# First batch's scores with tokens on partitions, its softmax without VectorE transposes, a float8 step that GpSimd may take

## The chip, the cores and the metric

The kernel runs on one core of a Trainium2 chip. The metric is the device time of one execution in microseconds (us). TensorE (PE), VectorE (DVE), ScalarE (ACT) and GpSimd (POOL) compute; SyncE (SP) issues the transfers. PEld stands for TensorE's loading of weights, which the profile lists apart from its matmuls.

## The reference

An attention block with 32 state tokens for each head feeds two MLPs. Sizes: 4 batches, 8 heads, 512 tokens, head width 64; then 2176 rows of 512, a first MLP of width 2048 and a second of width 1536.

```python
scores = scale * np.matmul(x, state.transpose(0, 1, 3, 2))
scores = scores - scores.max(-1, keepdims=True)
a = np.exp(scores)
a /= a.sum(-1, keepdims=True) + 1e-09
xread = np.matmul(a, state)
scores2 = scale * np.matmul(state, x.transpose(0, 1, 3, 2))
...
sread = np.matmul(a2, x)
x = concatenate([xread, sread])          # per head, then heads side by side
h = x @ w_in
g = np.where(h >= 1, h, np.where(h <= -1, 0.0, (h + 1) ** 2 / 4.0))
y = g @ w_out
out = ((y @ w_a) * (y @ w_b)) @ w_out2
```

All arrays are float32 or wider; the weights reach the chip as 8-byte words.

## The kernel before, in words

**Arithmetic.** A float32 operand is split into a rounded part (`hi`) and the rest (`lo`), both of the type float32r, and a product is made of three matmuls, hi·hi, hi·lo and lo·hi (`three`, `mms`, L378 to L393). Plain float32 matmuls are issued for the small products: scores, transposes, and the products with the state; the trace shows each of those as two matmuls and two weight loads. The two MLPs use a seven-product scheme of Strassen's kind.

**Weights.** `conv_steps` (L404) loads a block of 8-byte words and makes float32 of it in three steps: `copy` takes one byte of each word, a second step converts that byte through float8 (`upper` in the changed kernel; here always an ACT instruction), and `join` puts the bits together on DVE. For the first MLP's input weights, 512 columns (`c0`, `c1`) or 1024 columns (`c2` and all later ones) are converted at a time.

**Attention, batch 0.** Two head groups, `k` = 0 and 1, of four heads each. `a_qk(k)` makes the scores with the 32 state tokens on partitions. `a_soft(k)` (L619) is the softmax over the 32 states: DVE transposes the scores in 32x32 blocks (L635), takes the maximum (L636), POOL subtracts it (`spread`, L628), ACT exponentiates (L360), DVE sums (L639), adds 1e-9 (L642) and inverts (L647), POOL multiplies (L628), DVE transposes back (L649), ACT makes `hi` and DVE `lo` (L653). The same scores give the second softmax, over the tokens: `s_soft` (L704), `s_tr` (transposes by TensorE, L757) and `s_read` (L772). `w_steps` (L664) makes the product of state and input weights, which takes the place of `xread @ w_in`: the product of attention and that is the first MLP's hidden layer, six matmuls of 512 columns for each of its 16 row blocks `f` (`h_mm`, L813, traced at L385). `gate` applies the activation on ACT, POOL or ACT, and DVE.

**Order.** Every operation is recorded in `Flow.op` with costs for each engine that may do it, and `Flow.order` (L95) lays them out: the engine that can start first takes, of what is ready, the operation whose due time (`late`) is earliest, and the table `NUDGE` shifts the due times of single operations and excludes engines for some. TensorE's operations keep the order of the code unless they are marked `loose`. Each engine works through its own list in order. In `phase_one` (L1346) the head of batch 0 is written out by hand: while `flow.row` is a dictionary, operations of one engine are chained in that written order. `warm` (L864) issues matmuls whose result nobody reads: 11 at the start, then `FILL` = 12 and 10.

**Banks.** Eight PSUM banks: 0 to 3 for hidden blocks (the ring `four`), 4 and 5 together are the tile `lower` (scores), 6 and 7 the tile `upper` (state times weights).

Of the kernel before, what the change touches and what calls it, by code (L numbers as in the profile page):

```python
# [9 lines left out]
F32 = mybir.dt.float32  # L10
# [3 lines left out]
ALU = mybir.AluOpType  # L14
# [6 lines left out]
    64: (119,), 65: (2433,), 72: (638,), 78: (-4.5,), 79: (20.5, "POOL"), 90: (-9.5,), 92: (658.5,), 100: (78,),  # L21
    109: (-9,), 138: (69,), 163: (-32,), 196: (-9,), 219: (-12.5,), 304: (7.5,), 328: (6, "ACT"), 1010: (33,),
    1011: (30.5,), 1092: (10,), 1094: (-1.5,), 1096: (10,), 1103: (5.5,), 1138: (-5.5,), 1170: (10,),
    1172: (191.5,), 1182: (-1,), 1201: (-5,), 1208: (29.5,), 1211: (27,), 1213: (10.5,), 1217: (8,), 1235: (-4.5,),
    1278: (9.5,),
# [175 lines left out]
def attention_then_two_mlps(  # L201
# [116 lines left out]
    def bank(b):  # L318
        return ("P", b, b + 1)
# [84 lines left out]
    def conv_steps(src, k, stage, z, dst=None, by=("ACT",)):  # L404
# [28 lines left out]
        def copy(e):  # L433
# [4 lines left out]

        t = 0.18 + 0.00116 * n
# [5 lines left out]
            lambda: act(to, z, n, AF.Copy, regs(z), regs(z), t=t, saturate=False),  # L445
# [149 lines left out]
    def a_qk(k):  # L595
# [15 lines left out]
        op({"PE": 1.05}, emit, regs(d["st"], d["xld"]), [bank(b)], loose=k > 1)  # L611
# [7 lines left out]
    def a_soft(k, sub=("POOL",), mult=("POOL",), low=("DVE", "POOL")):  # L619
        d = qs[k]  # L620
        t1, b = d["t1"], sbank[k]
# [3 lines left out]
        def spread(engs, alu, v):  # L625
            op(
                {x: {"DVE": 0.7, "POOL": 1.1}[x] for x in engs},
                lambda e: eng(e).tensor_tensor(g32(t1()), g32(t1()), b32(v()), alu),  # L628
                regs(t1, v),
                regs(t1),  # L630
                port=True,
            )

        return [
            lambda: op({"DVE": 0.72}, lambda e: nc.vector.transpose(t1(), banks[b]), [bank(b)], regs(t1)),  # L635
            lambda: op({"DVE": 0.69}, lambda e: nc.vector.reduce_max(mx(), g32(t1()), axis=AX.X), regs(t1), regs(mx)),  # L636
            lambda: spread(sub, ALU.subtract, mx),
# [10 lines left out]
            lambda: spread(mult, ALU.mult, sm),  # L648
            lambda: op({"DVE": 0.71}, lambda e: nc.vector.transpose(d["at"](), t1()), regs(t1), regs(d["at"])),  # L649
            lambda: hi_of(hi, d["at"], 512, regs(d["at"]), regs(hi)),  # L650
# [3 lines left out]
                regs(d["at"], hi),  # L654
                regs(lo),
                port=True,
            ),
        ]

    def w_state(*args):  # L660
# [933 lines left out]
```

## Time and profile before

| | |
|---|---|
| median of 3 runs | 712.39 us (711.58 to 712.58) |
| the profiled execution | 711.84 us, of which 710.1 us are its span |
| TensorE matmul busy | 697.3 us, 98% of the span |
| TensorE weight loads busy | 653.9 us |
| VectorE, ScalarE, GpSimd busy | 556.5, 421.1, 105.3 us |
| mean granted TensorE clock | 0.998 of full speed |

Busy time is the time in which an engine had an instruction under way. In the page's 40 slices TensorE is at 9 tenths in every slice but the first (7) and the last (7), so what it does not do lies almost all in the first 18 us and some stretches behind them. "Idle before" in a row is the time that the engine stood still ahead of that instruction, and the name behind the arrow is what released it.

### The profile page before, as it was taken

The numbers are of one execution on the slowest core, as the hardware profiler recorded it, in microseconds if no ns is written. First come the engines' busy times: TensorE is split into PE (matmuls) and PEld (weight loads), VectorE is DVE, ScalarE is ACT, GpSimd is POOL, SyncE is SP. The second block draws the span as 40 slices with busy tenths as digits, with TensorE's granted clock in tenths as the row PEclk, the third lists the DMA queues.
The fourth block names the chain that finished last, engine by engine and source line by source line (L and its number), as shares of the span: only waits on it lengthen the run. The fifth ranks groups of instructions, "written<-read, shape, count | busy, mean of one in ns | idle before, by whom it ended". The sixth has DMA issues, their size and how long they took to land.

```text
span 710.1 us, 12246 instructions
## 1 busy us (share of the span) xinstructions
PE 697.3 (98%) x4818; PEld 653.9 (92%) x4818; DVE 556.5 (78%) x701; ACT 421.1 (59%) x622; POOL 105.3 (15%) x75
## 2 busy tenths in 40 slices
PE   7799999999999999999999999999999999999997
PEld 6366767889999999999999999999999999999997
DVE  6898879898997787899998686756536888987760
ACT  4888888697445455666666666455325536544440
POOL 3445768792000000000000000000000000000000
PEclk9999999999999999999999999999999999999999
DMA  8879977395674165142445767363631348454201
GB/s 345 346 247 325 330 279 264 104 386 162 207 252 150 63 196 190 54 143 106 135 149 178 243 221 245 117 195 109 203 135 42 106 145 287 127 174 146 79 30 44
DMA packets 75449, 128.92 MB, mean 182 GB/s; under 512 B 5632, under 2 KB 51200, under 8 KB 75392
## 3 DMA queue, kind: packets, MB, share of 16 engines
q1 hardware_dynamic: 75392, 128.15, 53.7%
q8 instruction: 37, 0.61, 0.3%
q14 instruction: 20, 0.16, 0.1%
HBM read 84.87 MB, written 43.25 MB: 180 GB/s over the span
## 4 chain that ended last, share of the span: by engine, by line
PE 89%; DMA 4%; DVE 3%; ACT 2%; issue 1%; POOL 0%; DVEq 0%; POOLq 0%; ACTq 0%
PE bank L385 82%; PE bank L843 2%; PE upper L674 2%; DMA f<-in_w_dram 2%; DMA g_d<-fs 1%; PE lower L772 1%; DMA f<-g_d 1%; ACT f L360 1%; PE bank L867 1%; DVE f L918 1%; DVE rh L370 1%; DVE r L370 1%; DMA f<-x_d 0%; PE lower L540 0%; PE lower L757 0%
## 5 line engine op out<-in xcount | busy, mean ns | idle before, releaser
L385 PE MATMUL bank<-rh,r 128*128 128x352 f32 (+2 forms) x1398 | 222.4, 316 | 0.9 <-ACT f L360 0.5
L385 PEld LDWEIGHTS bank<-rh,r 128*128 128x128 f32 x1398 | 215.9, 189 | 1.7 <-DVE rh L370 0.7
L360 ACT ACTIVATE f<-bank 128x368 f32<-128x368 f32 (+3 forms) x183 | 82.4, 454 | 124.5 <-PE bank L385 123.7
L385 PE MATMUL bank<-r,r 128*128 128x368 f32 (+1 forms) x960 | 156.2, 315 | 0.0
L385 PEld LDWEIGHTS bank<-r,r 128*128 128x128 f32 x960 | 147.8, 188 | 0.1
L360 ACT ACTIVATE rh<-f 128x736 fp32r<-128x736 f32 (+5 forms) x120 | 100.4, 846 | 75.8 <-PE bank L385 65.7
L370 DVE TENSOR_TENSOR f<-bank,f 128x368 f32<-128x368 f32 (+2 forms) x168 | 85.8, 517 | 72.3 <-PE bank L385 68.0
L370 DVE TENSOR_TENSOR rh<-f,rh 128x736 fp32r<-128x736 f32 (+5 forms) x120 | 119.2, 1002 | 25.5 <-ACT rh L360 25.0
L385 PE MATMUL bank<-r 128*128 128x512 f32 (+1 forms) x582 | 121.1, 360 | 4.5 <-ACT r L360 2.0
L385 PEld LDWEIGHTS bank<-r 128*128 128x128 f32 x582 | 94.7, 190 | 30.0 <-issue 8.4
L370 DVE TENSOR_TENSOR r<-f,r 128x768 fp32r<-128x768 f32 (+6 forms) x85 | 94.3, 1122 | 15.6 <-ACT r L360 15.6
L360 ACT ACTIVATE r<-f 128x768 fp32r<-128x768 f32 (+6 forms) x85 | 80.2, 953 | 39.7 <-PE bank L385 17.9
L385 PE MATMUL bank<-rh 128*128 128x352 f32 (+2 forms) x564 | 93.5, 318 | 0.1
L385 PEld LDWEIGHTS bank<-rh 128*128 128x128 f32 x564 | 88.4, 189 | 1.2 <-DVE f L370 0.6
L918 DVE TENSOR_TENSOR f<-f 128x256 f32<-128x256 f32 (+6 forms) x106 | 83.3, 804 | 6.1 <-DMA f<-p_d 5.0
L385 PE MATMUL bank<-r,rh 128*128 128x368 f32 (+1 forms) x480 | 80.3, 315 | 0.0
L385 PEld LDWEIGHTS bank<-r,rh 128*128 128x128 f32 x480 | 74.3, 188 | 0.0
L360 ACT ACTIVATE f<-f 128x1024 fp8e5<-128x1024 f32 (+1 forms) x43 | 48.0, 1122 | 2.0 <-POOL f L437 1.7
L435 ACT ACTIVATE f<-f 128x512 fp8e5<-128x512 fp8e5 (+1 forms) x28 | 28.1, 1004 | 20.3 <-DMA f<-in_w_dram 14.6
L448 DVE SCALAR_TENSOR_TENSOR f<-f 128x1024 uint32<-128x1024 uint32 (+1 forms) x34 | 34.0, 999 | 6.9 <-ACT f L360 6.8
L793 ACT ACTIVATE f<-bank,half 128x512 f32<-128x512 f32 x40 | 27.4, 691 | 9.1 <-PE bank L385 5.5
L807 DVE SCALAR_TENSOR_TENSOR f<-f,bank 128x512 f32<-128x512 f32 x40 | 26.5, 678 | 4.9 <-ACT f L800 3.5
(65 smaller groups left out, 432.8 us busy)
## 6 DMA issues: line engine op xcount, KB each, us to landing
f<-in_w_dram SPq DMA_DIRECT2D x25, 1024.0 KB, 6.2
f<-g_d SPq DMA_DIRECT2D x36, 368.0 KB, 4.9
f<-p_d SPq DMA_DIRECT2D x17, 768.0 KB, 4.9
g_d<-f SPq DMA_DIRECT2D x40, 256.0 KB, 5.1
f<-in_w_dram SPq DMA_DIRECT2D x18, 512.0 KB, 4.1
p_d<-f SPq DMA_DIRECT2D x48, 184.0 KB, 2.0
g_d<-fs SPq DMA_DIRECT2D x28, 256.0 KB, 4.8
f<-g_d SPq DMA_DIRECT2D x16, 352.0 KB, 4.7
```

The source lines that it names most:

```text
L360: lambda e: nc.scalar.activation(dst(), src(), func, **{k: (v() if callable(v) else v) for k, v in kws.items()}),
L370: op({"DVE": t_tt(n)}, lambda e: nc.vector.tensor_tensor(dst(), a(), b(), alu), rd, wr, port=port)
L385: nc.tensor.matmul(o, w, x, start=first and k == 0, stop=last and k == n - 1, skip_group_check=onto)
L435: nc.scalar.activation(to(), of(), AF.Copy, saturate=False)
L448: lambda e: nc.vector.scalar_tensor_tensor(out(U32), words_of(1, U32)(), 5, z(U32), ALU.logical_shift_right, ALU.bitwise_or),
L674: nc.tensor.matmul(banks[ab[q]][o : o + NS, :cols].rearrange("p (f x) -> p f x", x=P), st[q]()[64 * h : 64 * h + 64, NS * j : NS * j + NS] ...
L772: nc.tensor.matmul(banks[4][64 * e2 : 64 * e2 + 64, o : o + NS], xn()[:, c * 256 + p * 128 + e2 * 64 : c * 256 + p * 128 + (e2 + 1) * 64], ...
L793: lambda e: nc.scalar.activation(g(), h(), AF.Relu, bias=half[:, 0:1], scale=0.5),
L807: lambda e: nc.vector.scalar_tensor_tensor(g(), g(), 1.0, h(), ALU.min, ALU.max),
L843: nc.tensor.matmul(banks[b][:, P * i : P * i + P], w[:, P * c : P * c + P], xs()[:, P * c : P * c + P], start=c == 0, stop=c == 3,)
L867: nc.tensor.matmul(banks[3][:, :128], ident, ident, start=True, stop=True)
L918: lambda e: eng(e).tensor_tensor(dst(), a(), b(), alu),
```

## The change

Scores of batch 0 are also made with the tokens on partitions, by a new function `t_qk(k)`: for `k` = 0 eight matmuls of 64 moving columns, for `k` = 1 sixteen of 32 columns, all with 128x128 weights taken from `x`. They go to banks 0 and 1. The softmax reads them there: the maximum and the subtraction are DVE instructions with a PSUM operand, both `STREAM_TRANSPOSE` pairs are gone, the multiplication may be DVE's or POOL's, and the way back is four TensorE transposes for each `k` (`back`), after which `hi` and `lo` read PSUM. `a_qk(0)` and `a_qk(1)` stay, for the second softmax. The float8 step may be done by POOL wherever the copy step lists POOL. `flow.row` is `None`, so the head's order comes from due times; the hand-written list is changed, `NUDGE` is another table, and the ring `four` starts with bank 2.

```diff
 NUDGE = {
-    64: (119,), 65: (2433,), 72: (638,), 78: (-4.5,), 79: (20.5, "POOL"), 90: (-9.5,), 92: (658.5,), 100: (78,),
...
+    24: (136,), 30: (31.5,), 31: (29,), 32: (16.5,), 36: (63,), 37: (70,), 39: (19,), 40: (29.5,),
...
+        def upper(e):
+            if e == "ACT":
+                nc.scalar.activation(to(), z(), AF.Copy, saturate=False)
+            else:
+                eng(e).tensor_copy(to(), z(), saturate=False)
...
-            lambda: act(to, z, n, AF.Copy, regs(z), regs(z), t=t, saturate=False),
+            lambda: op({x: c for x, c in (("ACT", t), ("POOL", 0.2 + 0.0012 * n)) if x == "ACT" or x in by}, upper, regs(z), regs(z), port=True),
...
-        op({"PE": 1.05}, emit, regs(d["st"], d["xld"]), [bank(b)], loose=k > 1)
+        op({"PE": 0.55}, emit, regs(d["st"], d["xld"]), [bank(b)], loose=True)
+
+    def t_qk(k):
+        d = qs[k]
+
+        def emit(e):
+            for c in range(4):
+                for j in range(0, 4, 2 - k % 2):
+                    o, m = P * c + NS * (j ^ (k % 2)), NS * (2 - k % 2)
+                    nc.tensor.matmul(
+                        banks[k][:, o : o + m],
+                        d["xld"]()[:, 512 * (j // 2) + P * c : 512 * (j // 2) + P * c + P],
+                        d["st"]()[:, NS * j : NS * j + m],
+                        start=True,
+                        stop=True,
+                    )
+
+        op({"PE": 1.1}, emit, regs(d["st"], d["xld"]), [bank(k)])
...
+        def back(e):
+            for c in range(4):
+                nc.tensor.transpose(banks[k][:, P * c : P * c + P], t1()[:, P * c : P * c + P], ident)
...
-            lambda: op({"DVE": 0.72}, lambda e: nc.vector.transpose(t1(), banks[b]), [bank(b)], regs(t1)),
-            lambda: op({"DVE": 0.69}, lambda e: nc.vector.reduce_max(mx(), g32(t1()), axis=AX.X), regs(t1), regs(mx)),
-            lambda: spread(sub, ALU.subtract, mx),
...
+            lambda: op(
+                {"DVE": 0.66}, lambda e: nc.vector.reduce_max(mx(), g32(banks[k]), axis=AX.X), [bank(k)], regs(mx)
+            ),
+            lambda: op(
+                {"DVE": 0.68},
+                lambda e: nc.vector.tensor_tensor(g32(t1()), g32(banks[k]), b32(mx()), ALU.subtract),
+                [bank(k)] + regs(mx),
                 regs(t1),
-                port=True,
-            )
...
-            lambda: spread(mult, ALU.mult, sm),
-            lambda: op({"DVE": 0.71}, lambda e: nc.vector.transpose(d["at"](), t1()), regs(t1), regs(d["at"])),
-            lambda: hi_of(hi, d["at"], 512, regs(d["at"]), regs(hi)),
...
+            lambda: op({"PE": 0.5}, back, regs(t1), [bank(k)], loose=True),
+            lambda: hi_of(hi, lambda: banks[k], 512, [bank(k)], regs(hi)),
+            lambda: tt(lo, lambda: banks[k], lambda: hi(F32), ALU.subtract, 512, [bank(k)] + regs(hi), regs(lo)),
...
-    four, six = Ring([0, 1, 2, 3]), Ring([4, 5, 6, 7, 2, 3] * 2 + [6, 7, 2, 3])
+    four, six = Ring([2, 3, 0, 1]), Ring([4, 5, 6, 7, 2, 3] * 2 + [6, 7, 2, 3])
...
-        a_qk(0)
-        a_qk(1)
...
+        t_qk(0)
+        t_qk(1)
...
-        flow.row = {}
+        flow.row = None
...
-            s0[tr], s0[mx], s0[sub], s1[tr], s1[mx], s1[sub], c0[copy], s0[exp], c0[byte], s1[exp], s0[sm], c0[join],
...
+            s0[mx], s0[sub], s1[mx], s1[sub], c0[copy], s0[exp], c0[byte], s1[exp], s0[sm], s0[eps], s0[rec], s0[mult],
+            c0[join], lambda: a_qk(0), lambda: a_qk(1), v0[prod], s0[back], lambda: warm(FILL[1]), c1[copy], v0[top], v0[top1],
```

What this does to the order. The first place is TensorE's list from its first instruction to the first hidden block. Before (L867 is `warm`, L603 `a_qk`, L674 the product of state and weights, L385 a hidden block):

```order
L867 MATMUL bank_70<-ident 128x128 x11
L603 MATMUL lower<-fs 32x512 x8
L867 MATMUL bank_70<-ident 128x128 x12
L674 MATMUL upper<-fs 32x128 x8
L867 MATMUL bank_70<-ident 128x128 x10
L385 MATMUL bank_67<-r_65 128x512 x6
```

Now (L890 is `warm`, L608 `a_qk`, L625 `t_qk`, L697 the product of state and weights, L649 `back`, L384 a hidden block; banks 67 to 70 are banks 0 to 3):

```order
L890 MATMUL bank_70<-ident 128x128 x11
L608 MATMUL lower<-fs 32x512 x4
L625 MATMUL bank_67<-fs 128x64 x8
L608 MATMUL lower<-fs 32x512 x4
L625 MATMUL bank_68<-fs 128x32 x16
L890 MATMUL bank_70<-ident 128x128 x12
L697 MATMUL upper<-fs 32x128 x8
L890 MATMUL bank_70<-ident 128x128 x10
L649 MATMUL bank_68<-ident,fs 128x128 x4
L649 MATMUL bank_67<-ident,fs 128x128 x4
L384 MATMUL bank_69<-r_65 128x512 x6
```

Both `t_qk` stand ahead of the first fill, and each behind the `a_qk` of its group; `back` stands between the second fill and the first hidden block.

The second place is TensorE's list behind that, around the first transposes of the second softmax (`s_tr`, L757 before). Before:

```order
L674 MATMUL upper<-fs 32x128 x8
L385 MATMUL bank_68<-r_65 128x512 x6
L674 MATMUL upper<-fs 32x256 x8
L385 MATMUL bank_69<-r_65 128x512 x6
L674 MATMUL upper<-fs 32x512 x8
L385 MATMUL bank_70<-r_65 128x512 x6
L757 MATMUL lower<-ident,fs 128x128 x4
L385 MATMUL bank_67<-r_65 128x512 x6
L757 MATMUL lower<-ident,fs 128x128 x4
```

Now (`s_tr` is L780):

```order
L697 MATMUL upper<-fs 32x128 x8
L384 MATMUL bank_70<-r_65 128x512 x6
L697 MATMUL upper<-fs 32x256 x8
L780 MATMUL lower<-ident,fs 128x128 x4
L697 MATMUL upper<-fs 32x512 x8
L780 MATMUL lower<-ident,fs 128x128 x4
L384 MATMUL bank_67<-r_65 128x512 x6
L384 MATMUL bank_68<-r_65 128x512 x6
```

Both `s_tr` have moved ahead of the third hidden block; before, two blocks stood ahead of the first of them and three ahead of the second.

The third place is DVE's list at the head. Before (L635 and L649 are the transposes, L636 the maximum, L639 the sum, L448 `join`, L642 and L647 the small steps, L370 `lo` of state times weights):

```order
L635 STREAM_TRANSPOSE fs<-lower 128x512
L636 TENSOR_REDUCE fs<-fs 128x16
L635 STREAM_TRANSPOSE fs<-lower 128x512
L636 TENSOR_REDUCE fs<-fs 128x16
L639 TENSOR_REDUCE fs<-fs 128x16
L448 SCALAR_TENSOR_TENSOR fs<-f_66 128x512
L642 TENSOR_SCALAR fs<-fs 128x16
L647 RECIPROCAL fs<-fs 128x16
L639 TENSOR_REDUCE fs<-fs 128x16
```

Now (L653 is the maximum, L657 the subtraction, L453 `join`, L662 the sum, L665 and L670 the small steps):

```order
L653 TENSOR_REDUCE fs<-bank_67 128x16
L657 TENSOR_TENSOR fs<-bank_67,fs 128x512
L653 TENSOR_REDUCE fs<-bank_68 128x16
L657 TENSOR_TENSOR fs<-bank_68,fs 128x512
L453 SCALAR_TENSOR_TENSOR fs<-f_66 128x512
L662 TENSOR_REDUCE fs<-fs 128x16
L665 TENSOR_SCALAR fs<-fs 128x16
L662 TENSOR_REDUCE fs<-fs 128x16
L665 TENSOR_SCALAR fs<-fs 128x16
L670 RECIPROCAL fs<-fs 128x16
```

`join` of the first weights, on which the first product of state and weights waits, stands behind the second group's subtraction, as it stood behind the second group's maximum and the first group's sum before.

## Rows read from the trace of the kernel before

**Rows 1.** The page, busy time, share and instructions of each engine.

```profile
PE 697.3 (98%) x4818; PEld 653.9 (92%) x4818; DVE 556.5 (78%) x701; ACT 421.1 (59%) x622; POOL 105.3 (15%) x75
```

**Rows 2.** TensorE's waits, first 60 us: waiting, releaser, total us, times, longest.

```profile
PE bank L385 <- ACT r L360: 2.0, 3, 0.8
PE bank L385 <- DVE r L370: 1.6, 2, 0.9
...
PE lower L757 <- ACT fs L740: 1.0, 1, 1.0
PE bank L385 <- DVE r L653: 0.9, 1, 0.9
PE lower L603 <- DVE fs L635: 0.8, 1, 0.8
PE upper L674 <- DVE fs L448: 0.4, 1, 0.4
```

**Rows 3.** Windows: length, busy us of PE, PEld, DVE, ACT, POOL, clock, DMA.

```profile
15.00:20.00 5.00, 3.04 (x24) 1.52 (x24) 5.00 (x7) 3.65 (x7) 3.18 (x2) 1.00 1.03 396
20.00:25.00 5.00, 2.88 (x24) 1.47 (x25) 4.07 (x10) 4.88 (x9) 1.36 (x2) 1.00 1.03 411
25.00:30.00 5.00, 4.97 (x26) 1.96 (x24) 3.94 (x5) 3.03 (x4) 1.35 (x1) 0.66 1.03 410
```

**Rows 4.** Timeline of TensorE: start us, us, instruction, idle before and releaser.

```profile
5.53 1.06 PE L603 MATMUL lower<-fs 64*32 64x512 f32 x8
...
11.73 0.45 PE L674 MATMUL upper<-fs 64*32 64x128 f32 x16 [0.36 <-DVE fs L448]
...
20.46 1.19 PE L385 MATMUL bank<-r 128*128 128x512 f32 x4 [0.76 <-DVE r L370]
...
24.64 1.75 PE L385 MATMUL bank<-r 128*128 128x512 f32 x4 [0.87 <-DVE r L370]
26.32 1.96 PE L674 MATMUL upper<-fs 64*32 64x512 f32 x16
...
33.67 1.09 PE L674 MATMUL upper<-fs 64*32 64x512 f32 x16
```

**Rows 5.** Weight loads by shape, whole span: busy us, mean ns of one.

```profile
L843 PEld LDWEIGHTS bank<-fs 128*128 128x128 f32 x128 | 14.6, 192 | 1.8 <-issue 1.7
...
L772 PEld LDWEIGHTS lower<-fs 128*64 128x64 f32 x256 | 7.8, 138 | 2.4 <-ACT fs L360 1.7 <-ACT r L360 0.4 <-issue 0.4
```

**Rows 6.** Small float32 matmuls by shape, whole span: busy us, mean ns.

```profile
L843 PE MATMUL bank<-fs 128*128 128x128 f32 x128 | 15.0, 277 | 0.0
...
L772 PE MATMUL lower<-fs 128*64 128x32 f32 x256 | 8.2, 223 | 0.5 <-ACT fs L360 0.5
L757 PE MATMUL lower<-ident,fs 128*128 128x128 f32 x32 | 4.7, 279 | 1.1 <-ACT fs L740 1.0
```

**Rows 7.** Timeline of DVE at the head.

```profile
6.66 0.72 DVE L635 STREAM_TRANSPOSE fs<-lower 128x512 f32<-128x512 f32 x1 [3.63 <-PE lower L603]
7.42 0.69 DVE L636 TENSOR_REDUCE fs<-fs 128x16 f32<-128x512 f32 x1
...
11.60 0.16 DVE L642 TENSOR_SCALAR fs<-fs 128x16 f32<-128x16 f32 x1
...
12.63 0.65 DVE L642 TENSOR_SCALAR fs<-fs 128x16 f32<-128x16 f32 x1
```

**Rows 8.** Timeline of POOL at the head.

```profile
8.18 1.05 POOL L628 TENSOR_TENSOR fs<-fs 128x512 f32<-128x512 f32 x1 [6.88 <-DVE fs L636]
...
14.70 1.35 POOL L437 COPY f<-f 128x1024 uint8<-128x1024 uint8 x1
```

**Rows 9.** Timeline of ACT: first softmax's exponentials, a scaling of the second.

```profile
9.26 0.63 ACT L360 ACTIVATE fs<-fs 128x512 f32<-128x512 f32 x1 [0.63 <-POOL fs L628]
...
11.16 0.63 ACT L360 ACTIVATE fs<-fs 128x512 f32<-128x512 f32 x1 [0.59 <-POOL fs L628]
...
29.30 0.71 ACT L740 ACTIVATE fs<-fs 128x512 f32<-128x512 f32 x1
```

More of the change, by code (lines that the diff above doesn't have):

```diff
@@ L20 @@
 NUDGE = {
-    64: (119,), 65: (2433,), 72: (638,), 78: (-4.5,), 79: (20.5, "POOL"), 90: (-9.5,), 92: (658.5,), 100: (78,),
[L22 to L25, printed above, removed]
+    24: (136,), 30: (31.5,), 31: (29,), 32: (16.5,), 36: (63,), 37: (70,), 39: (19,), 40: (29.5,),
+    47: (-98.5, "POOL"), 54: (-5,), 58: (-55,), 66: (128,), 90: (-31,), 108: (4,), 122: (-3.5,), 137: (9.5, "DVE"),
+    142: (36,), 185: (18.5,), 224: (7.5,), 312: (16,), 647: (3, "POOL"), 1010: (27.5,), 1011: (23,), 1076: (6.5,),
+    1091: (-9.5,), 1110: (3,), 1138: (-8,), 1205: (-5,), 1211: (0.5,), 1261: (10,), 1263: (2.5,),
 }
@@ L647, in a_soft @@
             lambda: op({"DVE": 0.25}, lambda e: nc.vector.reciprocal(sm(), sm()), regs(sm), regs(sm), port=True),
[L648 to L650 removed]
             lambda: op(
[L652 to L655 removed]
+                {"DVE": 0.7, "POOL": 1.1},
+                lambda e: eng(e).tensor_tensor(g32(t1()), g32(t1()), b32(sm()), ALU.mult),
+                regs(t1, sm),
+                regs(t1),
                 port=True,
             ),
+            lambda: op({"PE": 0.5}, back, regs(t1), [bank(k)], loose=True),
+            lambda: hi_of(hi, lambda: banks[k], 512, [bank(k)], regs(hi)),
+            lambda: tt(lo, lambda: banks[k], lambda: hi(F32), ALU.subtract, 512, [bank(k)] + regs(hi), regs(lo)),
         ]
@@ L1361, in phase_one @@
         warm(WARM)
-        a_qk(0)
-        a_qk(1)
-        s0 = a_soft(0, ("POOL",), ("POOL",), ("DVE",))
-        s1 = a_soft(1, ("POOL",), ("POOL",), ("DVE",))
+        t_qk(0)
+        t_qk(1)
+        s0, s1 = a_soft(0), a_soft(1)
         first_w.append(len(flow.ops))
         v0, v1, v2 = w_steps(0, 0, 0, 1), w_steps(0, 0, 1, 2), w_steps(0, 0, 2, 4)
-        flow.row = {}
-        tr, mx, sub, exp, sm, eps, rec, mult, back, high, low = range(11)
+        flow.row = None
+        mx, sub, exp, sm, eps, rec, mult, back, high, low = range(10)
         copy, byte, join = range(3)
@@ L1373, in phase_one @@
         for f in (
-            s0[tr], s0[mx], s0[sub], s1[tr], s1[mx], s1[sub], c0[copy], s0[exp], c0[byte], s1[exp], s0[sm], c0[join],
-            s0[eps], s0[rec], s0[mult], v0[prod], lambda: warm(FILL[1]), c1[copy], v0[top], v0[top1], c1[byte],
-            s1[sm], s1[eps], s1[rec], s1[mult], v0[rest], v0[rest1], s0[back], s0[high], s1[back], s1[high], s0[low],
-            c2[copy], s1[low], c1[join], c2[byte],
+            s0[mx], s0[sub], s1[mx], s1[sub], c0[copy], s0[exp], c0[byte], s1[exp], s0[sm], s0[eps], s0[rec], s0[mult],
+            c0[join], lambda: a_qk(0), lambda: a_qk(1), v0[prod], s0[back], lambda: warm(FILL[1]), c1[copy], v0[top], v0[top1],
+            s0[high], c1[byte], s1[sm], s1[eps], s1[rec], s1[mult], v0[rest], v0[rest1], s0[low], s1[back], s1[high],
+            c1[join], s1[low], c2[copy], c2[byte],
         ):
```

14 lines of the change are left out of this document (4 added, 10 removed).

## The prediction

> **What bounds the kernel now.** I read the page first: TensorE is busy for 697.3 of 710.1 us [rows 1], so the time is TensorE's work and its standing still. Then TensorE's waits: in the first 60 us it waits 6.7 us [rows 2], not counting the 1.4 us before its first instruction, which the change doesn't touch. All of that lies between 7 and 34 us; behind it TensorE has a queue of ready work, and a late head is not made good. Most of it [rows 2] is of one kind: a hidden block waits for `hi` from ACT or `lo` from DVE of a product that TensorE has just made. The windows show what that costs besides: TensorE is busy for 3.04 and 2.88 of 5 us between 15 and 25 us, and in the next 5 us the granted clock is 0.66 [rows 3], full speed and half speed mixed (2.4 and 1.2 GHz). At the half clock four matmuls of a hidden block take 1.75 us where the same four took 1.19, and eight products with the state 1.96 where they take 1.09 [rows 4]: 0.56 + 0.87 = 1.43 us lost. So the head holds 6.7 + 1.4 us that a better order could win, about 1.1% of the time; the rest of the kernel nothing that this change touches.
>
> The sum is made against the profiled execution, 711.84 us; the median of the runs shown is 0.55 us above it, which I add at the end. 0.2%, 1.4 us, is about what a measurement of this kernel can tell from no change.
>
> **TensorE's new work: `t_qk`.** Eight and sixteen matmuls, seen twice each in a trace as all plain float32 ones are: 16 + 32 = 48 passes, each with its own load of 128x128 weights. No row shows 128 weight columns with only 32 or 64 moving ones, so I bound the pass. From above: 128x128 with 128 moving columns is 15.0 us for 128 passes [rows 6], 0.117 us each, 5.6 us for 48. From below: 64 weight columns with 32 moving ones is 8.2 us for 256 [rows 6], 0.032 us each; taking that for 32 moving columns and twice it for 64 gives 32 x 0.032 + 16 x 0.064 = 2.0 us. Which of the two depends on what a pass waits for. A load of 128 weight columns takes 192 ns, one of 64 takes 138 [rows 5]: 54 ns for 64 columns more, so 108 ns of a 128-column load grow with the columns. Loads of full-width weights have one array to go to, so I take 0.11 us for each pass whatever moves: 16 x 0.11 = 1.8 us for `k` = 0, 32 x 0.11 = 3.5 us for `k` = 1, **5.3 us**. That is the term on which the forecast rests.
>
> A rule speaks against it. The Trainium skill, "TensorE: Matmul & The Clock Gate", section "Back-to-back issue gap", gives a floor of about 60 cycles, 25 ns, between matmuls of 1 to 64 columns; by it the 48 passes would be an estimated 1.2 us. The same section says that this gap leaves out the weight loads. In this trace the only matmuls that come near it have 32- or 64-column weights.
>
> **Does it lie on the path?** It does, by the order. TensorE does `a_qk(0)`, `t_qk(0)`, `a_qk(1)`, `t_qk(1)` in that order, an `a_qk` being 1.06 us and starting at 5.53 [rows 4]: 5.5 + 1.0 + 1.8 + 1.0 + 3.5 = 12.8 us for the end of the second scores. DVE's list then has the second maximum and subtraction, and behind them `join`, about 0.7 us each like its other steps on 512 columns [rows 7]: 12.8 + 3 x 0.7 + hops = 15.1 us. The first product of state and weights waits for that `join` and started at 11.73 [rows 4]; it is 3.4 us late. The 24 passes of the first fill stand behind `t_qk(1)` and end about 0.4 us later still, so nothing covers the new work: before, the fill covered a wait.
>
> What the softmax saves is smaller. Before, the first exponential starts at 9.26 [rows 9], 3.7 us after `a_qk(0)`: transpose 0.72, maximum 0.69 [rows 7], POOL's subtraction 1.05 [rows 8]. Now it is 1.0 + 1.8 + tail 0.2 + 0.69 + 0.7 + hops = 4.5 us, at about 10.0. For the second, 12.8 + 0.2 + 1.4 + hops = 14.5 us against 11.16 [rows 9].
>
> **Transposes back.** Eight on TensorE at 4.7 us / 32 = 0.15 us [rows 6] where they stand alone, 0.11 in a row: 0.9 to 1.2 us, **0.9** taken. They replace two DVE transposes of about 0.7 us each, which TensorE's fill covered in part.
>
> **Waits.** Gone are the wait of the second `a_qk` for DVE (0.8) and the one for `join` (0.4, now under the fill) [rows 2]. The pair at the first hidden block stays at about 1.2 us, since `hi` and `lo` of its weights still come from ACT and DVE one after the other; so does the pair at the second, 1.3. The pair at the third block and the 1.0 us at the second `s_tr` go, for `s_tr` now stands ahead of the third block. In their place TensorE meets the first `s_tr` earlier: two exponentials, two small DVE steps, a scaling at 0.71 [rows 9], in all 2.5 us behind the second softmax's maximum, less the product of state and weights that covers 0.6: 1.9 us. Sum 4.4 for 6.7: **2.3 us less**.
>
> **Clock.** The stretch from the first product of state and weights to `s_tr` has work and waits in about the proportion of 15 to 25 us [rows 3], so I expect the half clock again, 3 to 4 us later; since the waits are then fewer and longer, I take half of 1.43 us as won, **0.7**, with 0 and 1.43 as bounds.
>
> **POOL.** It loses two subtractions and one product of 1.05 us and gets a float8 step of 1024 columns for most blocks. No row shows that step on POOL; its byte copy of the same size takes 1.35 us, and two of its 512-column steps would be 2.1 [rows 8]. I take 1.4 and no cost, because ACT, which did the step, and POOL both have idle time there [rows 3]. It isn't free of risk: a 16-element DVE step took 0.65 us instead of 0.16 while a POOL instruction ran beside it [rows 7]. Price of the upper bound: four such collisions and a step that is 0.7 us late twice, about 2 us.
>
> **Sum.** 5.3 + 0.9 - 2.3 - 0.7 = +3.2 us; 715.0 us for a profiled execution, and with 0.55 us **715.6 us** for the median. Its own range: pass at 0.117 (+0.3), clock not won (+0.7), POOL's price (+1 of 2) up to 717.6; the clock won whole (-0.7) and the waits shorter by 1 us down to 713.9.
>
> **Rivals.** *Columns set the pass.* If weight loads hide behind each other, `t_qk` is 2.0 us or less, and the sum is 2.0 + 0.9 - 2.3 - 0.7 = -0.1: 712.3 us, within 0.2%. For it: 0.032 us a pass for 32 moving columns. Against it: the growth of a load with its columns [rows 5]. By the rule on the gap it would be an estimated -0.9 us, the same side. Chance 0.2.
>
> *The queue fills behind the late start (faster).* While TensorE is on `t_qk`, the weights go on landing and ACT and DVE go on converting them; if by 15 us the blocks behind are ready, the waits [rows 2] don't come back and the clock doesn't fall: 5.3 + 0.9 - 6.7 - 1.4 = -1.9, 710.5 us. It decides from the point at which less than about 1 us of waits is left. For it: DVE is busy for 5.00 of 5 us between 15 and 20 us [rows 3], so a share of its work would be out of the way. Against it: the waits are for `hi` and `lo` of a product that TensorE itself has just made, and no head start on weights shortens those. Chance 0.15.
>
> *POOL becomes what is waited for.* The float8 step is the slower one and holds up DVE: the sum and its 2 us, some of it more than once: 717 to 719 us. The Trainium skill, "GPSIMD Engine Reference", section "1. Specifications", says that POOL shares its SBUF interfaces with VectorE and contends with two-port modes and two-input instructions; the 0.65 us step agrees [rows 7]. Chance 0.1.
>
> The forecast has 0.55. Faster 0.15, within 0.2% (711.0 to 713.8) 0.2, slower 0.65. The range takes in the columns rival and part of the others: 711.0 to 718.0 us.
>
> **What would show it.** Right: in the changed trace `t_qk(1)` takes over 3 us, about 0.11 us from pass to pass, with the first product of state and weights behind 15 us, and the waits of TensorE in the first 60 us sum to 4 to 5 us. Wrong: `t_qk` together under 3 us; or a first hidden block before 18 us; or no half clock; or waits of POOL's float8 results on TensorE's path.

## The result, and the profile after

The changed kernel takes 716.06 us (median of 8 runs, 714.73 to 719.68), the kernel before 711.61 us (8 runs, 710.9 to 714.98): ratio 1.0066, 95% interval 1.0040 to 1.0092, 4.45 us slower. The forecast was 715.6. In two of those eight runs, and in one of six later ones, the mean granted clock was 0.992 or 0.993 and the time 719.5 to 719.7, in the other eleven 0.998 to 1.0 and 714.7 to 718.0. The profiled execution took 716.08 us at a clock of 1.0, 4.24 more than the profiled one of before.

The page of the changed kernel, busy time, share and instructions of each engine (before: [rows 1]):

```profile
PE 702.4 (98%) x4874; PEld 660.1 (92%) x4874; DVE 555.9 (78%) x702; ACT 417.8 (58%) x620; POOL 101.8 (14%) x72
```

TensorE is busy for 5.1 us more while the span grew by 4.2, so it stands idle about 0.9 us less. The timeline of TensorE at the head (before: [rows 4]; columns: start us, us, instruction, idle before and releaser) says where the work went:

```profile
6.61 2.00 PE L625 MATMUL bank<-fs 128*128 128x64 f32 x16
8.54 1.06 PE L608 MATMUL lower<-fs 64*32 64x512 f32 x8
9.53 3.76 PE L625 MATMUL bank<-fs 128*128 128x32 f32 x32
13.13 2.92 PE L890 MATMUL bank<-ident 128*128 128x128 f32 x24
15.98 0.45 PE L697 MATMUL upper<-fs 64*32 64x128 f32 x16
16.36 2.50 PE L890 MATMUL bank<-ident 128*128 128x128 f32 x20
19.06 1.20 PE L649 MATMUL bank<-ident,fs 128*128 128x128 f32 x8 [0.20 <-POOL fs L673]
```

L625 is `t_qk`. From its start to the start of what follows it takes 1.93 us for 16 passes and 3.60 for 32: 0.121 and 0.113 us a pass, 5.5 us together, though a pass of the second moves half the columns of the first. TensorE is loading weights for nearly all of it (busy us, mean ns of one):

```profile
L625 PEld LDWEIGHTS bank<-fs 128*128 128x128 f32 x48 | 5.5, 192 | 1.7 <-issue 1.7
```

The first product of state and weights (L697) starts at 15.98 instead of 11.73. The transposes back (L649) are 1.2 us; the trace shows each of the eight once, so what is said of two matmuls and two weight loads ahead of the prediction doesn't hold for transposes.

TensorE's waits in the first 60 us (before: [rows 2]; waiting, releaser, total us, times, longest):

```profile
PE lower L780 <- ACT fs L763: 1.4, 1, 1.4
PE bank L384 <- ACT r L359: 1.3, 2, 0.7
PE upper L697 <- DVE r L369: 1.0, 1, 1.0
PE bank L384 <- DVE r L369: 0.7, 2, 0.4
PE bank L649 <- POOL fs L673: 0.2, 1, 0.2
```

That is 4.6 us for 6.7. The same view from 60 us to the end, where the kernel before has three waits of together 1.4 us:

```profile
PE bank L384 <- DVE fs L830: 1.1, 1, 1.1
PE bank L384 <- ACT f L359: 0.8, 2, 0.5
PE bank L384 <- DVE rh L369: 0.8, 2, 0.6
```

So 1.3 us more behind the head in this execution (0.3 us in another one of the same kernel, e5). The windows of the stretch in which the forecast expected the half clock (length, busy us of PE, PEld, DVE, ACT, POOL, clock, DMA):

```profile
20.00:25.00 5.00, 3.31 (x27) 1.56 (x25) 4.70 (x8) 3.82 (x7) 2.61 (x2) 1.00 0.98 356
25.00:30.00 5.00, 2.45 (x24) 1.27 (x24) 4.93 (x11) 4.87 (x10) 1.64 (x3) 1.00 1.00 409
```

TensorE is busy for 2.45 of 5 us, less than in those of [rows 3], and the clock is 1.00 there and in the windows behind it. The sum in one execution: t_qk +5.5, transposes back +1.2, waits in the head -2.1, waits behind it +1.3, clock -1.4: +4.5, where the spans differ by 4.2.

### The profile page after: what moved, and what is told of

The parts are those of the page before. It is cut to its first block, busy times and chain, and to the rows that moved or that the text cites. A ratio compares the mean times of both kernels' runs of the same rounds, so it can differ in the third digit from the quotient of the medians.

```text
span 714.3 us, 12342 instructions
## 1 busy us (share of the span) xinstructions
PE 702.4 (98%) x4874; PEld 660.1 (92%) x4874; DVE 555.9 (78%) x702; ACT 417.8 (58%) x620; POOL 101.8 (14%) x72
## 4 chain that ended last, share of the span: by engine, by line
PE 89%; DVE 4%; DMA 3%; ACT 1%; issue 1%; POOL 1%; SPq 0%; POOLq 0%; DVEq 0%; ACTq 0%
PE bank L384 82%; DMA f<-in_w_dram 2%; PE bank L866 2%; PE upper L697 2%; PE lower L795 1%; DVE rh L369 1%; PE bank L625 1%; DMA f<-g_d 1%; DVE fs L453 1%; PE bank L890 1%; DVE f L941 1%; DVE r L369 1%; ACT f L440 0%; PE lower L780 0%; POOL fs L825 0%
## 5 line engine op out<-in xcount | busy, mean ns | idle before, releaser
L384 PE MATMUL bank<-rh,r 128*128 128x352 f32 (+2 forms) x1398 | 222.5, 316 | 0.6 <-ACT f L359 0.5
L384 PEld LDWEIGHTS bank<-rh,r 128*128 128x128 f32 x1398 | 215.8, 189 | 1.5 <-ACT f L359 0.7
L384 PE MATMUL bank<-r,r 128*128 128x368 f32 (+1 forms) x960 | 156.1, 315 | 0.0
L384 PEld LDWEIGHTS bank<-r,r 128*128 128x128 f32 x960 | 147.9, 188 | 0.0
L384 PE MATMUL bank<-r 128*128 128x512 f32 (+1 forms) x582 | 120.3, 359 | 3.1 <-ACT r L359 1.3
L384 PEld LDWEIGHTS bank<-r 128*128 128x128 f32 x582 | 94.5, 189 | 28.3 <-issue 5.9
L384 PE MATMUL bank<-rh 128*128 128x352 f32 (+2 forms) x564 | 94.0, 319 | 0.9 <-DVE rh L369 0.6
L941 DVE TENSOR_TENSOR f<-f 128x256 f32<-128x256 f32 (+7 forms) x108 | 86.5, 817 | 6.4 <-DMA f<-p_d 3.6
L384 PEld LDWEIGHTS bank<-rh 128*128 128x128 f32 x564 | 88.3, 189 | 2.7 <-DVE rh L369 0.9
L384 PE MATMUL bank<-r,rh 128*128 128x368 f32 (+1 forms) x480 | 80.3, 315 | 0.0
L384 PEld LDWEIGHTS bank<-r,rh 128*128 128x128 f32 x480 | 74.3, 188 | 0.0
L434 ACT ACTIVATE f<-f 128x512 fp8e5<-128x512 fp8e5 (+1 forms) x30 | 30.9, 1029 | 22.2 <-DMA f<-in_w_dram 17.7
L453 DVE SCALAR_TENSOR_TENSOR f<-f 128x1024 uint32<-128x1024 uint32 (+1 forms) x34 | 34.1, 1002 | 5.2 <-ACT f L440 4.3
L440 ACT ACTIVATE f<-f 128x512 fp8e5<-128x512 f32 (+1 forms) x34 | 35.8, 1056 | 1.7 <-POOL f L436 1.4
L825 POOL TENSOR_TENSOR f<-f 128x512 f32<-128x512 f32 x22 | 27.8, 1271 | 22.3 <-ACT f L816 22.3
```

Of the source, the lines that this page charges most:

```text
L384: nc.tensor.matmul(o, w, x, start=first and k == 0, stop=last and k == n - 1, skip_group_check=onto)
L434: nc.scalar.activation(to(), of(), AF.Copy, saturate=False)
L440: nc.scalar.activation(to(), z(), AF.Copy, saturate=False)
L453: lambda e: nc.vector.scalar_tensor_tensor(out(U32), words_of(1, U32)(), 5, z(U32), ALU.logical_shift_right, ALU.bitwise_or),
L825: eng(e).tensor_tensor(g(), g(), g(), ALU.mult)
L941: lambda e: eng(e).tensor_tensor(dst(), a(), b(), alu),
```

## The experiments

Two theories go in. Mine: `t_qk` costs what its 48 weight loads take TensorE, all of it on the path, and nothing else of the change is worth much. Against it: the columns set the pass; or the queues of the other engines fill while TensorE is on `t_qk`, and pay it back; or GpSimd's float8 step costs. Each run was compared with the kernel before, run beside it on the same chip (medians there 711.1 to 712.0 us). "At the full clock" means the runs of a kernel whose mean granted clock was 0.999 or more.

### The pass and the path: e1, e6, e3, e2, e9

e1_double, `t_qk` twice:

```diff
-            for c in range(4):
+            for c in (0, 1, 2, 3, 0, 1, 2, 3):
```

> The changed kernel with every matmul of t_qk issued twice, in the same place; the second writes the same numbers over the first, so nothing of the computation changes. Theory (a pass is set by the load of its 128 weight columns, and all of t_qk lies on the path, because the head's waits are for hi and lo of products that TensorE has just made and no later start shortens them): t_qk goes from 5.5 to 11.1 us, the first product of state and weights from 15.98 to about 21.4, TensorE's waits in the head stay at 4 to 4.6 us, and the time goes from 716.1 to 721.0 to 721.6 us. Rival (the queue fills behind a late start): ACT and DVE get ahead while TensorE is on t_qk, 2 us or more of the 4.6 us of waits go, and the time is 717.5 to 719.5. Rival (columns set the pass): t_qk 4 us or less, 713 to 715 for the kernel with a single t_qk to begin with; the trace of the changed kernel already speaks against it.

e6_double_wide, the same with all 128 columns moving in every pass:

```diff
-            for c in range(4):
+            for c in (0, 1, 2, 3, 0, 1, 2, 3):
                 for j in range(0, 4, 2 - k % 2):
...
-                        banks[k][:, o : o + m],
+                        banks[k][:, P * c : P * c + P],
...
-                        d["st"]()[:, NS * j : NS * j + m],
+                        d["st"](),
```

> As e1_double (every matmul of t_qk twice), but each matmul moves all 128 columns of the state instead of 32 or 64, with the same weights and the same number of passes; the scores that come out are of mixed heads, so the first batch's attention is of other numbers. Theory for the pass (the load of 128 weight columns sets it): 96 passes at 0.113 to 0.120 us, 11 to 11.5 us together at the full clock, no more than in e1_double. Rival (columns set it): two to four times as long. On the clock: in e1_double it fell to 0.60 and 0.50 between 15 and 25 us, in the middle of t_qk(1). If it is the thin use of the array by 32 moving columns that lets the clock fall, it stays at 1.0 here and the time is 721 to 722; if it falls in any long stretch that waits for weight loads, it falls here too and the time is 725 to 727.

e1 took 725.89 us (ratio 1.0206, 1.0192 to 1.0221), e6 722.42 (1.0149, 1.0131 to 1.0166); the changed kernel run beside e6 took 715.83. The second `t_qk` in the timeline of e1, and then the windows over it:

```profile
11.81 10.04 PE L625 MATMUL bank<-fs 128*128 128x32 f32 x64
```
```profile
15.00:20.00 5.00, 5.00 (x31) 5.00 (x30) 0.00 (x0) 0.00 (x0) 0.00 (x0) 0.60 0.52 191
20.00:25.00 5.00, 5.00 (x24) 5.00 (x25) 3.04 (x5) 1.30 (x2) 1.03 (x1) 0.50 0.35 108
```

The same row and the first of these windows in e6:

```profile
12.59 7.41 PE L624 MATMUL bank<-fs 128*128 128x128 f32 x64
```
```profile
15.00:20.00 5.00, 5.00 (x47) 5.00 (x47) 0.00 (x0) 0.00 (x0) 0.00 (x0) 1.00 0.61 228
```

Four times the columns in the same number of passes: 7.41 / 64 = 0.116 us a pass at the full clock. So the columns do not set the pass, and that rival is out. Nor is it a fixed price of any pass: with 64 weight columns one takes 0.032 us [rows 6]. What is left is the load of the 128 weight columns.

In e1 the granted clock falls to its half level inside that row (0.60 over one window, 0.50 over the next). The row and the fill behind it take 4.9 us more than in e6, and e1 missed its 721.6 by 4. In e6, where the engine does the same loads and moves more columns, the clock stayed at 1.00; its two runs at the full clock have a median of 722.0, forecast 721 to 722.

e6 is 6.6 us slower than the changed kernel for 5.5 us of passes, and its waits in the head are 4.7 us for 4.6: here nothing of a later start is paid back. In the profiled executions most of the other 1.1 us stands ahead of `t_qk`, which starts at 7.83 us for 6.80 in e5.

e3_eight, `t_qk(1)` in eight matmuls:

```diff
+            turned = qs[1]["at"].sub(0, P)
+            if k < 1:
+                s, t = (v().rearrange("p (c q n) -> p c q n", q=2, n=NS) for v in (qs[1]["st"], turned))
+                for q in range(2):
+                    nc.gpsimd.tensor_copy(t[:, :, q, :], s[:, :, 1 - q, :])
+            st = turned if k else d["st"]
...
-                for j in range(0, 4, 2 - k % 2):
+                for j in range(0, 4, 2):
...
```

> The changed kernel with t_qk(1) done like t_qk(0), in 8 matmuls with 64 moving columns instead of 16 with 32; so that its heads come out in the exchanged order that the rest wants, GpSimd, which is idle then, first writes a copy of the state with the columns of each pair of heads exchanged (two copies of 128x64). The same is computed. Theory (loads set the pass): 16 passes of about 0.113 us fewer, t_qk(1) 3.76 to about 2.0 us, first product of state and weights near 14.2 to 14.8, time 716.1 - 1.8 = 714.3 (713.8 to 715). Rival (columns set the pass): the columns are the same, t_qk(1) stays near 3.7 us and the time at 716.

715.07 us (1.0056, 1.0043 to 1.0069), 1.0 less than the changed kernel by the medians, with intervals that overlap. `t_qk(1)` took 2.00 us for 3.76:

```profile
10.68 2.00 PE L630 MATMUL bank<-fs 128*128 128x64 f32 x16
```

The pass is confirmed, the 1.8 us in the time is not. In the profiled execution they do come off the path: from the start of `t_qk(0)` to the transposes back it takes 10.71 us for 12.45. But `t_qk(0)` itself starts at 7.76 us for 6.61, a late start that kernels without this edit show too (e6, e7, e8, e12).

e2_none, one matmul for each `t_qk`:

```diff
-            for c in range(4):
...
+            nc.tensor.matmul(banks[k], d["xld"]()[:, :P], d["xld"]()[:, :512], start=True, stop=True)
```

> The changed kernel with t_qk of each batch replaced by one matmul of 128 weight columns and 512 moving ones on the same data (about 0.5 us each), so the first batch's scores with tokens on partitions are not computed and its attention is of other numbers; softmax, transposes back and everything behind them run as before. Theory: 4.5 us come off TensorE ahead of everything and all of it is on the path as far as join lets it: first product of state and weights near 12 us, time 716.1 - 4 = 712 (711.5 to 713), about the kernel before. Rival (the late start was partly paid back by shorter waits): the waits in the head grow from 4.6 back to 6 us or more and the clock falls to its half level somewhere between 15 and 30 us; time 713.5 to 715. If it falls under 711, the rest of the change (the order, the softmax without VectorE transposes, GpSimd's step) is a gain that t_qk hides.

713.24 us (1.0023, 1.0013 to 1.0033), 2.8 less than the changed kernel. The two matmuls took 1.0 us each, not 0.5, so 3.5 us came off TensorE; the waits in the head did not grow (3.1 us), but the clock fell in the profiled execution, and all twelve runs are at 0.995 to 0.998:

```profile
20.00:25.00 5.00, 4.56 (x40) 2.27 (x38) 4.72 (x10) 3.37 (x9) 1.32 (x1) 0.50 1.04 414
```

The rival's clock came true, its waits did not, and the time lies between the two forecasts. It did not fall under 711, where I would have called the rest of the change a gain. But 2 us of `t_qk` and the half clock are still in it, so a gain of a microsecond or so in the rest is not ruled out.

e9_early, the same work on TensorE with the second scores some 3 us earlier:

```diff
...
-                        banks[k][:, o : o + m],
...
+            nc.tensor.matmul(banks[k], d["xld"]()[:, :P], d["xld"]()[:, :512], start=True, stop=True)
+            if k:
...
+                            banks[3][:, o : o + m],
...
```

> The changed kernel with t_qk's work on TensorE kept in amount and place, but its results early: each t_qk is one matmul of 128 weight and 512 moving columns on the same data (1.0 us, as in e2_none, so the first batch's attention is of other numbers), and behind the second one stand 16 matmuls, 32 passes, that nobody reads (3.8 us). TensorE is through with them at about 13.3 us, as with the true t_qk; VectorE has its scores at about 9.9 us instead of 13.2. Theory (t_qk costs what it takes TensorE): same time, 715 to 716.5, waits in the head 4.6 us. Rival (from e7, where the same 48 passes cost only about 1.3 us at the full clock, with VectorE already through with the scores: half or more of the cost is that VectorE starts the second softmax 3.3 us later and then runs without a pause to 45 us): waits in the head 1.5 to 3 us less, 712.5 to 714. In runs at a mean clock of 0.999 or more.

716.15 us (1.0061, 1.0048 to 1.0075), the changed kernel's time by the medians. The forecasts were for the full clock, and only one run of six is there: 714.70, between the two, and 3.6 us above the kernel before beside it (711.1 at the full clock), as e5 is 3.7 above. VectorE had its second scores at 10.18 us for 13.33 and stood idle later instead, behind the same chain; first the row of VectorE, then TensorE's waits:

```profile
17.36 0.49 DVE L369 TENSOR_TENSOR r<-upper,r 128x128 fp32r<-128x128 f32 x2 [2.68 <-ACT r L359]
```
```profile
PE lower L782 <- ACT fs L765: 1.4, 1, 1.4
PE bank L384 <- ACT r L359: 1.3, 2, 0.7
PE upper L699 <- DVE r L369: 1.0, 1, 1.0
PE bank L384 <- DVE r L369: 0.8, 2, 0.5
```

The waits are those of the changed kernel, 4.5 us for 4.6. That VectorE starts the second softmax late costs nothing that they show; in this order `t_qk` costs TensorE's time. In this execution (717.19 us) the clock fell behind the head, and the eight products with the state took 1.96 us as in [rows 4]; first the window, then the row:

```profile
30.00:35.00 5.00, 4.96 (x26) 2.81 (x27) 4.97 (x6) 2.22 (x3) 2.05 (x2) 0.50 0.76 297
```
```profile
30.04 1.96 PE L699 MATMUL upper<-fs 64*32 64x512 f32 x16 [0.97 <-DVE r L369]
```

### The same work in the old order: e7

e7_before_dead: the loop of `t_qk` at the end of `a_qk` in the kernel before, writing `banks[1 + k]`, which nobody reads there.

```diff
+            for c in range(4):
+                for j in range(0, 4, 2 - k % 2):
...
+                        banks[1 + k][:, o : o + m],
...
```

> The kernel before with the matmuls of t_qk added behind those of a_qk, for both halves of the first batch, into two banks that nobody reads there; everything else, order and softmax included, is the kernel before. Theory: 5.5 us more on TensorE, of which the 0.84 us wait of the second a_qk and the 0.36 us wait for join are covered; first product of state and weights at about 16 us for 11.73; behind it only the 0.86 us wait for the first softmax's lo goes, since the others are for products that TensorE has just made: 711.7 + 3.5 = 715.2 (714.5 to 716.5), 3.5 to 4 more if the clock falls in it. Rival (the queue fills behind a late start): the waits between 15 and 35 us nearly all go, and with them the half clock behind them: 712.5 to 713.5.

The median is 715.54 us (1.0046, 1.0029 to 1.0064), where I had expected it, and for another reason. Five of the twelve runs are at the full clock: 712.63 to 713.81, median 712.9, against 711.6 for the kernel before beside it: 1.3 us for 5.5 us of passes. The other seven, at 0.995 to 0.998, took 715.3 to 719.2. TensorE's waits in the first 60 us of the profiled one:

```profile
PE bank L385 <- ACT r L360: 1.3, 2, 0.8
PE lower L767 <- ACT fs L750: 1.1, 2, 0.9
PE bank L385 <- DVE r L370: 1.0, 2, 0.8
PE upper L684 <- DVE fs L448: 0.3, 1, 0.3
PE bank L385 <- DVE r L663: 0.2, 1, 0.2
```

3.9 us for 6.7 [rows 2]: the old order does get a late start paid back, by 2.8 us in its waits, where my theory had 2.1, and by 0.7 behind 60 us. What this execution loses besides, it loses to a late start (`a_qk(0)` at 6.35 us, for 5.53 in [rows 4]) and to the clock (0.88 and 0.78 from 10 to 20 us) in `t_qk(1)` and the fill, 3.76 and 2.94 us at the full clock:

```profile
10.54 4.10 PE L613 MATMUL bank<-fs 128*128 128x32 f32 x32
14.45 4.23 PE L877 MATMUL bank<-ident 128*128 128x128 f32 x24
```

So in the order of before, at the full clock, the rival's time came (712.5 to 713.5) and not mine; its step holds in part only, for between 15 and 35 us 4.0 us of 5.5 us of waits are left, and it had nearly none. For the order of the change mine holds. Beside the same kernel before, and at the full clock, e7 costs 1.3 us and the changed kernel 3.7 (e5): some 2.4 us of the change belong to its other parts, the transposes back (1.2) among them, and not to these passes alone.

### GpSimd's step: e4, e10

Both let ScalarE issue the step at the place where GpSimd had it; e4 for all but the first four of nine blocks, e10, with `> 0` in place of `> 4`, for all nine.

```diff
+    casts = []
...
         def upper(e):
-            if e == "ACT":
+            casts.append(e == "POOL")
+            if e == "ACT" or sum(casts) > 4:
```

> The changed kernel with the float8 step of GpSimd put back on ScalarE, at the same place in the order, for all but the first four of the nine blocks that GpSimd takes (so from about 60 us on). The same is computed. Theory from the trace of the changed kernel: TensorE's longest wait behind the head, 1.10 us at 82.9 us for a gate that VectorE finishes, goes back to GpSimd, whose square had stood behind a float8 step of 1.36 us; without that step the wait goes, 716.1 - 1.1 = 715.0 (714.6 to 715.4). Rival (the wait comes from the order of the gates, whoever does the step; or ScalarE is then late for another gate): same time, 715.8 to 716.4, with a wait of about 1 us somewhere between 60 and 130 us.

> The changed kernel with the float8 step of all nine blocks that GpSimd takes put back on ScalarE at the same place in the order. The same is computed. Theory (the forecast: GpSimd's step costs nothing that ends on TensorE, since ScalarE and GpSimd both have idle time there): same time, 714.5 to 716.5. Rival 1 (GpSimd's step costs: VectorE's join beside it takes 1.90 and 2.07 us instead of 1.21, and the hi and lo behind it are late): joins back at 1.2 us, the 0.97 us wait at 30 us shorter, 713.5 to 714.8. Rival 2 (it helps: ScalarE is the busier one between 20 and 35 us): 717 to 719.

e4 took 720.73 us (1.0125, 1.0108 to 1.0142), which neither forecast had. Its 1 us wait is still there, so the theory that the step made it is out: the copy of that block's bytes waits for its transfer, and whoever does the next step holds up the gate behind it. Most of the higher time comes from something else, in a stretch where e4 is instruction for instruction the changed kernel. The timeline of TensorE in e4, and then the windows there:

```profile
10.18 4.54 PE L627 MATMUL bank<-fs 128*128 128x32 f32 x32
14.53 5.42 PE L892 MATMUL bank<-ident 128*128 128x128 f32 x24
```
```profile
10.00:15.00 5.00, 5.00 (x38) 4.83 (x35) 0.94 (x2) 1.29 (x2) 0.00 (x0) 0.79 1.02 410
15.00:20.00 5.00, 5.00 (x32) 4.83 (x39) 4.09 (x8) 1.30 (x2) 1.96 (x2) 0.52 1.03 391
```

`t_qk(1)` and the fill behind it took 4.54 and 5.42 us instead of 3.76 and 2.92, 3.3 us lost to the half clock (three of four runs at 0.993). The clock is down a second time from 30 to 40 us (0.84 and 0.82).

e10 took 718.96 us (1.0110, 1.0086 to 1.0135), 717.1 at the full clock (two runs), 1.8 above the changed kernel's 715.3 (e5): my theory of the same time missed, and the second rival's 717 to 719 came. ScalarE's row of the step and TensorE's of the second hidden block:

```profile
23.90 1.32 ACT L442 ACTIVATE f<-f 128x1024 fp8e5<-128x1024 f32 x1
25.09 0.42 ACT L359 ACTIVATE r<-upper 128x128 fp32r<-128x128 f32 x2
```
```profile
25.40 1.69 PE L384 MATMUL bank<-r 128*128 128x512 f32 x6 [1.74 <-ACT r L359]
```

`hi` stands behind the step, and TensorE waits 1.74 us where it waited 0.56. Its waits behind `t_qk` are 5.4 us in the head for 4.6. Of the two long joins, one is as long as in the changed kernel (2.04 us; a gate's product on GpSimd runs beside it), the other went from 2.07 us beside the step to 1.21, in the changed kernel and then in e10:

```profile
31.19 2.07 DVE L453 SCALAR_TENSOR_TENSOR fs<-f 128x1024 uint32<-128x1024 uint32 x1
```
```profile
31.93 1.21 DVE L455 SCALAR_TENSOR_TENSOR fs<-f 128x1024 uint32<-128x1024 uint32 x1
```

The step does cost VectorE 0.86 us there, and TensorE has other work then. In this order the step on GpSimd is a gain of some 2 us by those two runs; the waits show 0.9 of it.

### Waits and clock: e5, e8, e11, e12

e5_after is the changed kernel unaltered.

> The changed kernel once more, unaltered, for its spread on the chip that runs the next three: in two of its eight first runs it took 719.6 us at a mean granted clock of 0.993, in the others 714.7 to 717.1 at 0.998 to 1.0. Theory (the granted clock falls to its half level in some executions during the long stretch of weight-load-bound passes and the fill behind it, and the same code does it or not): again two groups, 714.7 to 716.5 and about 719 to 721, the slower ones with the clock down somewhere between 10 and 25 us. Rival (the two slow ones were chance of another kind): all runs within 714.5 to 717.

715.83 us (1.0062, 1.0042 to 1.0082): 714.66 to 717.96, and one of 719.47 at 0.992; 715.3 at the full clock, 3.7 above before. The second group came again, as expected, but 717.96 lies between the two, and where the clock fell in the run of 719.47 is not known, since the profiled execution was at 1.0.

e8_before_fill puts idle matmuls into six waits of the kernel before (`pad` names the places):

```diff
+                if k in pad:
+                    for _ in range(2):
+                        nc.tensor.matmul(banks[3][:, :128], ident, ident, start=True, stop=True)
```

> The kernel before with idle work in six of TensorE's waits: two 128x128 matmuls on the identity into a bank that is free there (0.49 us) ahead of the two matmuls of each of the first three hidden blocks that waited 0.56 to 0.87 us for hi and lo. The same is computed. Theory on the clock (the half clock between 25 and 30 us follows the waits of 15 to 25 us, and costs 1.43 us there): with the waits filled the clock stays at 1.0, the four matmuls take 1.2 us again and the eight products 1.09: 711.7 - 1.4 = 710.3 (710.0 to 711.0). Rival (the fall has another cause, or the idle work delays what it stands ahead of): same time or up to 1 us more, the clock at about 0.66 again.

711.22 us against 711.97, ratio 0.9998 (0.9988 to 1.0008): no difference that can be told, where the theory had 1.4 us. The clock is where the theory wants it (25 to 30 us, for 0.66 in [rows 3]), and ten of eleven runs were at the full clock:

```profile
25.00:30.00 5.00, 4.57 (x35) 2.61 (x34) 4.07 (x7) 4.89 (x9) 1.37 (x1) 1.00 1.03 405
```

But 16 of the 23 runs of the kernel before beside it were at the full clock too, and e12, which fills no wait, has 1.00 in the same window, so the fill is not shown to do it. The 1.43 us of [rows 4] are lost in some executions only, and in the median there is little of them to win.

e11_lo_first and e12_before_lo_first move one VectorE instruction behind the `lo` of the third hidden block, the first in the changed kernel, the second in the kernel before:

```diff
...
     order = flow.order()
+    dve = [i for i in order if flow.ops[i][4] == "DVE"]
+    first = dve[dve.index(lows[0]) - 1]
+    order.remove(first)
+    order.insert(order.index(lows[1]) + 1, first)
...
```

`lows` holds the places of the two halves of that `lo`.

> The changed kernel with one instruction moved on VectorE and nothing else: the join of a weight block (27.51 us, 1.90 us long) goes behind the two subtractions that make lo of the state product for the third hidden block (29.33 us), instead of ahead of them. The same is computed. Theory (what stays of the waits in the new order is VectorE's queue: hi is ready at 27.8 us, lo comes only at 30.1 because the join stands ahead of it, and TensorE waits 0.97 us for it behind the state softmax's transposes): lo at 28.6 us, that wait goes, 716.0 - 1.0 = 715.0 at the full clock (714.0 to 715.4). Rival (the join is wanted as much: the next product with the state waits for its weights instead): the wait changes its name and the time stays at 715.5 to 716.5.

> The kernel before with one instruction moved on VectorE: the byte copy of a weight block (23.54 us, for which VectorE first stands 0.79 us, since its data have not landed) goes behind the two subtractions that make lo of the state product for the third hidden block (24.17 us). The same is computed. Theory: hi is ready near 22.9 us, so lo can be ready at about 23.8 instead of 24.6; TensorE's wait of 0.87 us there shrinks to 0.1 or 0.2, and with it the stretch that lets the clock fall: 711.7 - 0.7 = 711.0 (710.2 to 711.4), 1.4 more in those runs in which the clock fell. Rival (the copy is late then, and with it that block's float8 step, join and product): 711.5 to 712.5.

e11: 715.22 us (1.0062, 1.0042 to 1.0082). At the full clock it is 714.6, inside the theory's 714.0 to 715.4; but the kernel before beside it is 710.95 there, for 711.6 beside e5, so e11 is 3.6 us above it and e5 3.7: no better. e12: 711.45 (1.0004, 0.9991 to 1.0017), no better either. TensorE's next product with the state, in e11 and then in e12:

```profile
29.61 1.09 PE L697 MATMUL upper<-fs 64*32 64x512 f32 x16 [0.66 <-DVE fs L453]
```
```profile
27.09 1.09 PE L674 MATMUL upper<-fs 64*32 64x512 f32 x16 [0.91 <-DVE fs L448]
```

In both the wait for `lo` went (0.97 and 0.87 us) and one for the join came, at this product: VectorE's queue holds two results that TensorE wants next, and their order decides little more than the name of the wait. No version run here beats the kernel before by more than its interval.

## Why the prediction was right

| term | forecast | measured |
|---|---|---|
| `t_qk` | +5.3 | +5.5 |
| transposes back | +0.9 | +1.2 |
| waits of the first 60 us | -2.3 (4.4 left) | -2.1 (4.6 left) |
| clock | -0.7 | -1.4 in the profiled execution |
| GpSimd's step | 0 | a gain of some 2 against ScalarE in the same order (e10) |
| waits behind 60 us | not foreseen | +0.3 to +1.3 |
| sum | +3.2 | +4.2 (profiled), +4.45 (medians) |

**The pass.** Right, by the step on which it rested: the growth of a load with its columns [rows 5] gave 0.11 us, and the runs 0.113 to 0.121 at the full clock, whatever moves. The Trainium skill, "TensorE: Matmul & The Clock Gate", section "LDWEIGHTS (loading the stationary operand)", gives a load time in ns of the column count over 1.2, an estimated 107 ns for 128 columns: the trace comes near it (e6: 0.116 us a pass, 8% more). The floor of 25 ns in the Trainium skill, same page, section "Back-to-back issue gap", which spoke against the change being slow, is met by none of these passes.

**The path.** The first product of state and weights came at 15.98, for 15.1 and the fill's 0.4 behind it; the exponentials at 10.10 and 14.78, for 10.0 and 14.5. e6 shows, and e9 agrees as far as its one run at the full clock goes, that all of `t_qk` is TensorE's time on the path. The step "a late head is not made good" was too general: in the order of before most of the same 5.5 us is made good (e7). That the new order does not do it is shown; which of its moves takes that away was not settled. A part is visible: `s_tr` ahead of the third block waits 1.4 us for ScalarE's scaling, and the product behind it 1.0 us more for VectorE's `lo`. The sum of the waits came out (4.6 us for 4.4) by luck in its parts: the pairs at the first two blocks were 1.0 us each for 1.2 and 1.3, `s_tr` 1.4 for 1.9, and the 1.0 at the product and 0.2 at the transposes back were not foreseen.

**The clock.** This term was wrong for the profiled execution: no half clock behind 20 us, which the forecast had named as a sign against itself, so 1.4 us were won and not 0.7, and the waits behind 60 us, which were not in the sum, took 0.3 to 1.3 of it back. The place was not wrong altogether: in e9 and e10, variants of the changed kernel, the clock is 0.50 and 0.66 from 30 to 35 us. In e4 it falls earlier, in `t_qk(1)` and the fill, which are there the changed kernel's. So it falls in some executions and not in others, and before the change too, and what one profile loses to it is no term of the medians. At the full clock, where it is none, the two kernels are 3.7 us apart (e5), and the other terms with e5's waits give 5.5 + 1.2 - 2.1 + 0.3 = 4.9; the 1.2 us between are not accounted for. That the forecast lies within 0.5 us of the median is in part luck.

**GpSimd.** No cost, as in the sum, and the third rival is out: the step took 1.33 to 1.37 us in seven of nine blocks, for 1.4, and 2.18 in two; none of TensorE's waits ends with it.

```profile
23.73 1.33 POOL L442 CAST f<-f 128x1024 fp8e5<-128x1024 f32 x1 [2.17 <-DVE f L436]
35.21 2.18 POOL L442 CAST f<-f 128x1024 fp8e5<-128x1024 f32 x1 [2.97 <-DVE f L436]
```

## What to carry to other kernels

Count small matmuls by their weight loads, not their moving columns: a pass with 128 float32 weight columns costs some 0.115 us here whether 32 or 128 columns move. What work ahead of everything costs depends on the waits behind it: put it into the kernel as dead work, in the order as it is, and see how much of it the waits pay back before redesigning around it. And look at the granted clock of many runs before counting on what one profile loses to it.

## What had not been expected of the hardware

The same instructions ran at the full or the half clock from execution to execution. In e1 and e4 the engine had been on passes of 32 moving columns, each with a full weight load, when the clock fell to 0.60 and 0.79 over a window and 0.50 and 0.52 over the next; with 128 moving columns in e1's number of passes (e6) all four runs were at 0.998 to 1.0. What decides it for one execution of the changed kernel was not found. The 22 passes at the very start took 4.06 us in e10 and 5.06 in e6, with 1.00 in the clock's column for both; with them the whole head starts up to 0.9 us earlier or later (`a_qk(0)` at 5.41 us in e11 to 6.36 in e8). In the five executions with 5.06 (e3, e6, e7, e8, e12) `a_qk(0)` itself took 1.34 to 1.58 us for 1.06.
